# Second product of the first MoE with w_out as the stationary operand and 512 tokens moving

## The chip, the core and the metric

One NeuronCore of a Trainium2 chip runs the whole program in one launch. The metric is the device time of one execution in microseconds. Its engines run side by side, each in the order of its own list of instructions, and wait for one another by semaphores: TensorE (PE in the profile; PEld is its loading of stationary operands), VectorE (DVE), ScalarE (ACT), GpSimd (POOL) and SyncE (SP, which here only issues transfers). Matrix products are written to PSUM (eight banks of 512 float32 columns), everything else lives in SBUF or in device memory.

## The reference

Three stages follow each other. A linear attention with decay over 2 x 8 heads, 768 steps and head size 48 gives 1536 rows of 384 numbers. A dense layer then maps them through 2048 hidden values. Last comes a top-1 mixture of 8 experts.

```python
# stage 2: x is 1536 x 384
h = x @ w_in                                            # 384 x 2048
g = np.maximum(h, 0.0) + alpha * np.minimum(h, 0.0)
x = g @ w_out                                           # 2048 x 384
# stage 3: 8 experts, capacity 384 rows each
logits = x @ w_gate
expert_idx = np.argmax(logits, axis=1)
gate_w = softmax(logits)[row, expert_idx]
# rows go to their expert in order of the row number, up to the capacity
y = np.maximum(disp @ w1, 0.0) @ w2                     # 384 x 1024, 1024 x 384
out[i] = gate_w[i] * y[expert_idx[i], pos[i]]           # 0 for rows over the capacity
```

## The kernel before

The 1536 rows are treated as three blocks of four tiles of 128 rows. The attention turns each tile into x, transposed and split into a high and a low float32r part (`xT`), so that three products of parts stand for one float32 product (`PASS`: high x high, high x low, low x high).

The dense layer walks over 48 slices: for each of the three blocks, 16 slices of 128 hidden columns (`moe1_slice`, slice number g). In a slice TensorE makes the hidden values of 512 rows, nine matmuls with 512 moving columns (`moe1_first`, L599). ScalarE and VectorE apply the activation and split the result into `gh` and `gl` (128 hidden columns x 512 rows). Two slices later comes the second product (`moe1_second`, L584): for each of the four row tiles, a 128 x 128 piece of `gh` or `gl` is the stationary operand and a 128 x 384 piece of w_out moves; twelve matmuls a slice add into four PSUM banks `acc`, one for each row tile, with rows as partitions. TensorE's list is: hidden values of slice g, second product of slice g - 2, then whatever small work (attention of later tiles, routing of the block before) has been hung on the slice in the lists `work`.

When a block is done, its four banks are copied to `rows` by ScalarE (`evac`, L425). Routing then needs the logits. For each row tile TensorE transposes three pieces of `rows` (L431, the bank `px2`), a copy brings them to SBUF as `x2T` (L435), and six small matmuls against w_gate give 8 logits a row (L446, tile `pl`). For the first two blocks these steps are spread over the slices of the next block (`ROUTE_AT`). VectorE then picks the expert (`choose`, L454 to L466, one-hot `oh`), TensorE counts the rows of each expert before each row (`count`, L500, tile `pc`), VectorE works out the weight and the destination row (`weigh`, L475 to L488, and `place`, L506 to L515, destination `sl`), and GpSimd scatters each tile of 128 rows to the buffer `disp` in device memory by an indirect transfer (`scatter`, L522).

The last block has no later slices to hide in. Its routing is written out by hand after the loop (L1067 to L1117), in two halves of two row tiles, TA and TB, which share TensorE with `Early`: a product of expert 0 with 128 rows that are already there (tiles `eh_f`, `pht_f`, `ey_f`). After it come six matmuls whose result nobody reads (`keep_warm`, L756, tile `warm_e`). SP then loads the scattered rows of expert 0 (`load_rows`, L644), TensorE transposes them (`prep`, L658, tile `pd`), and the eight experts follow one after another (`expert`, L775 and L799), each while the weights of the next one are being split.

Of the kernel before, what the change touches and what calls it, by code (L numbers as in the profile page):

```python
# [18 lines left out]
P = 128  # L19
# [4 lines left out]
def kernel(  # L24
# [291 lines left out]
    ROUTE_AT = ((2, 4, 7, 10, 12, 13, 14),) * (NBLK - 2) + ((2, 3, 4, 5, 6, 7, 8),)  # L316
# [98 lines left out]
    def routing_steps(blk, R, s0, SUB, before=()):  # L415
# [7 lines left out]
        def evac(s):  # L423
            def f():
                nc.scalar.copy(R[:, s0 + s, 0:DM], accs[(blk, s0 + s)])  # L425
            return f

        def logit(s):
            pt = bank(f"px2_{nm}_{s}", "acc" if end else "att")
            for c in range(DC):  # L430
                nc.tensor.transpose(pt[:, c * P:(c + 1) * P], R[:, s0 + s, c * P:(c + 1) * P], ident)  # L431
            pool, tag = ((p1, "x2T"), (p2, "cv"), (p2, "cv"), (p1, "x2T"))[s0 + s if end else 0]
            T[s] = pool.tile([P, DC, P], F32, tag=tag, name=f"x2T{nm}_{s}")
            src = pt[:, 0:DM].rearrange("p (c t) -> p c t", c=DC)
            return lambda: (nc.vector.tensor_copy if end and s0 + s < 2 else nc.scalar.copy)(T[s], src)  # L435

        def logit_mm(s):
            if s == 0 and end:
                T["pl"] = bank(f"pl{nm}")
                T["lg"] = T["pl"][:, 0:SUB * E].rearrange("p (s e) -> p s e", s=SUB)  # L440
            elif s == 0:
                T["lg"] = p2.tile([P, SUB, E], F32, tag="lg", name=f"lg{nm}")
            pl = T["pl"][:, s * E:(s + 1) * E] if end else bank(f"pl{nm}_{s}")[:, 0:E]
            for c in range(DC):
                for x in range(2):
                    nc.tensor.matmul(pl[64 * x:64 * x + 64], T[s][:, c, 64 * x:64 * x + 64], wg[:, c, :],  # L446
                                     start=(c == 0), stop=(c == DC - 1), skip_group_check=True)
            return (lambda: None) if end else lambda: nc.vector.tensor_copy(T["lg"][:, s, :], pl)
# [116 lines left out]
        T["logit"], T["logit_mm"] = logit, logit_mm  # L565
        ev = [evac(s) for s in range(SUB)]
        T.update(choose=choose, weigh=weigh, count=count, place=place, scatter=scatter, total=total)
        steps = [pair(s) for s in range(SUB + 1)] + [lambda: weave(choose()), settle]
# [4 lines left out]
    gs = {}  # L573

    def moe1_second(fts, subs=None):
        blk = fts[0] // NFT
        for s in range(SIZES[blk]) if subs is None else subs:
            for g in fts:
                ft = g % NFT
                wout = moe1_w(ft // 2)[1]  # L580
                if ft == 0:
                    accs[(blk, s)] = ps_acc.tile([P, DM], F32, tag="acc", name=f"acc{blk}_{s}")
                for n, (a, b) in enumerate(PASS):
                    nc.tensor.matmul(accs[(blk, s)], gs[g][a][:, s * P:(s + 1) * P], wout[b][:, ft % 2, :],  # L584
                                     start=(ft == 0 and n == 0), stop=(ft == NFT - 1 and n == 2))
# [17 lines left out]
    def moe1_slice(g, work):  # L603
# [22 lines left out]
        if 2 <= g < NBLK * NFT - 1:  # L626
            moe1_second([g - 2])
# [18 lines left out]

    def claim(e):

        dT[e] = [p2.tile([P, DC, STRIDE], F32R, tag=("xh", "xl")[x], name=f"d{x}_{e}") for x in range(2)]
# [102 lines left out]
    def keep_warm(name, where, n, a, b):  # L752

        pt = bank(name, where)
        for _ in range(n):
            nc.tensor.matmul(pt[:, 0:b.free_size()], a, b, start=True, stop=True)  # L756
# [98 lines left out]
    with tc.manual_schedule():  # L855
# [190 lines left out]
        for blk in range(NBLK - 1):  # L1046
            def evac(blk=blk):
                ev, rt, _ = routing_steps(blk, rows_of(blk), 0, SIZES[blk])
# [20 lines left out]
        evA, rtA, TA = routing_steps(NBLK - 1, R, 0, 2)  # L1069
        evB, rtB, TB = routing_steps(NBLK - 1, R, 2, 2, before=(TA,))  # L1070
        L = [lambda T=T, s=s: T["logit"](s)() for T in (TA, TB) for s in range(2)]
        M = [lambda T=T, s=s: T["logit_mm"](s)() for T in (TA, TB) for s in range(2)]
        ev = evA + evB
        moe1_second([g - 2])
        moe1_second([g - 1], range(n - 1))
        for s in range(n - 1):
            moe1_second([g], [s])
            ev[s]()
        L[0]()
        moe1_second([g - 1], [n - 1])  # L1080
        L[1]()
        moe1_second([g], [n - 1])
        ev[3]()
        M[0]()
        L[2]()
        M[1]()
        L[3]()
        M[2]()
        early.hidden(0, 0, 1)
        weave(TA["choose"]())  # L1090
        TA["count"]()
        M[3]()
        early.hidden(0, 1, 9)
        weave(TA["weigh"](), TA["place"]())
        TA["scatter"]()
        weave(TB["choose"]())
# [9 lines left out]
        TB["total"]()  # L1106
# [7 lines left out]
        keep_warm("warm_e", "h", 6, early.d[0][:, 0, :], exp_w(0, 0)[0][:, 0, :])  # L1114
# [42 lines left out]
```

## Time and profile before

| | |
|---|---|
| median of three runs | 466.42 us (465.99 to 467.51) |
| profiled execution, its own time | 466.23 us |
| its span on the core | 464.5 us |
| mean granted TensorE clock | 0.989 of full |
| TensorE busy | 437.4 us (94% of the span) |
| VectorE, ScalarE, GpSimd busy | 271.0, 208.2, 157.7 us |

The span runs from the first to the last instruction of the program; the time of an execution is 1.7 us more. A row of the timeline gives the start in us from the start of the span, how long the row lasts, the engine, the source line, the operation, the tile written and the tiles read (stationary and moving operands are both named after the arrow), the shapes, and how many equal instructions stand in the row; in brackets is the idle time of the engine before it and what ended that. Matmuls overlap in the pipeline, so the pace of matmuls is read from start to start of rows, not from durations.

### The profile page before, as it was taken

To read this page: it belongs to the slowest core of one execution; us is meant where nothing else is said; L and a number is where in the kernel's file an instruction comes from. 1 tells how busy PE (TensorE), PEld (TensorE's weight loads), DVE (VectorE), ACT (ScalarE), POOL (GpSimd) and SP (SyncE) were. 2 spreads that over 40 slices of the span, in tenths; PEclk is the share of its full clock that TensorE was granted. 3 is DMA by queue.
4 is the path that set the end of the run, shared out by engine and by line. 5 is a ranking of instruction groups with operands and counts; after the bars stand their busy time and mean duration, and the time that the engine had idled before them with its cause. 6 is when DMAs were issued, how large, how long until landed. Compare 5 with 4: busy or idle time off the path is not lost. (4 is left out here: it accounts for less than half of the span.)

```text
span 464.5 us, 7861 instructions
## 1 busy us (share of the span) xinstructions
PE 437.4 (94%) x3039; PEld 385.1 (83%) x3039; DVE 271.0 (58%) x470; ACT 208.2 (45%) x344; POOL 157.7 (34%) x138
## 2 busy tenths in 40 slices
PE   7977799699899999999999999999999999999995
PEld 6766699588788988989988888987988889898884
DVE  6998998999753444445333665354463535452651
ACT  1236634354344333323244444336473646553761
POOL 6855457464440231100300030033343515241660
PEclk9999979989999999999999999999999999999999
DMA  6999950649610207101700020018956556580200
GB/s 129 229 281 250 318 157 4 183 158 361 172 30 15 52 2 233 57 0 43 299 1 1 0 87 0 1 56 290 382 178 239 188 169 212 172 271 35 72 10 25
DMA packets 70605, 62.28 MB, mean 134 GB/s; under 512 B 41935, under 2 KB 58239, under 8 KB 70561
## 3 DMA queue, kind: packets, MB, share of 16 engines
q1 hardware_dynamic: 68832, 57.29, 41.1%
q0 software_dynamic: 1728, 4.40, 2.5%
q8 instruction: 28, 0.46, 0.4%
q14 instruction: 17, 0.13, 0.1%
HBM read 49.99 MB, written 12.62 MB: 135 GB/s over the span
## 5 line engine op out<-in xcount | busy, mean ns | idle before, releaser
L584 PE MATMUL acc<-wm,gh 128*128 128x384 f32 x384 | 102.0, 347 | 0.5 <-POOL wm L368 0.5
L599 PE MATMUL h<-xh,wm 128*128 128x512 f32 (+1 forms) x294 | 86.2, 402 | 4.4 <-DVE gl L622 4.4
L618 DVE SCALAR_TENSOR_TENSOR h<-ng,sign,h 128x512 f32<-128x512 f32 x48 | 36.1, 752 | 68.2 <-ACT ng L615 68.2
L584 PEld LDWEIGHTS acc<-wm,gh 128*128 128x128 f32 x384 | 69.9, 191 | 4.7 <-POOL wm L368 0.8
L775 PE MATMUL eh<-we,d 128*128 128x512 f32 x252 | 65.1, 403 | 4.5 <-PEq L847 3.2
L584 PE MATMUL acc<-wm,gl 128*128 128x384 f32 x192 | 65.4, 341 | 0.0
L599 PEld LDWEIGHTS h<-xh,wm 128*128 128x128 f32 x294 | 52.6, 190 | 14.2 <-issue 2.8
L615 ACT ACTIVATE ng<-h,slope 128x512 f32<-128x512 f32 x48 | 33.1, 689 | 60.1 <-PE h L599 60.0
L775 PEld LDWEIGHTS eh<-we,d 128*128 128x128 f32 x252 | 45.7, 188 | 15.5 <-issue 4.4
L619 ACT CAST gh<-h 128x512 fp32r<-128x512 f32 x48 | 28.1, 586 | 60.8 <-DVE h L618 60.8
L674 ACT CAST we<-re 128x768 fp32r<-128x768 f32 x64 | 50.6, 839 | 9.6 <-DMA re<-in_moe_w_dram 6.8
L677 POOL TENSOR_TENSOR we<-re,we 128x768 fp32r<-128x768 f32 x21 | 40.6, 1932 | 38.5 <-ACT we L674 32.2
L790 DVE TENSOR_TENSOR hl<-pht,hh 128x512 fp32r<-128x512 f32 x28 | 19.4, 692 | 51.6 <-ACT hh L789 49.8
L368 POOL TENSOR_TENSOR wm<-rm,wm 128x768 fp32r<-128x768 f32 x16 | 32.2, 2013 | 47.4 <-ACT wm L367 43.6
L799 PE MATMUL ey<-we,hh 128*128 128x384 f32 x224 | 48.1, 346 | 0.0
L677 DVE TENSOR_TENSOR we<-re,we 128x768 fp32r<-128x768 f32 x43 | 40.3, 965 | 11.9 <-ACT we L674 8.9
L522 POOL DMA_INDIRECT disp<-rows,sl x12 | 12.6, 1051 | 99.9 <-DVE run L543 64.4
L599 PE MATMUL h<-xl,wm 128*128 128x512 f32 (+1 forms) x147 | 42.1, 395 | 0.1
L622 DVE TENSOR_TENSOR gl<-h,gh 128x512 fp32r<-128x512 f32 x48 | 33.0, 687 | 15.6 <-ACT gh L619 15.6
L799 PEld LDWEIGHTS ey<-we,hh 128*128 128x128 f32 x224 | 37.8, 189 | 0.3 <-ACT hh L789 0.3
L584 PEld LDWEIGHTS acc<-wm,gl 128*128 128x128 f32 x192 | 36.6, 191 | 0.0
L599 PEld LDWEIGHTS h<-xl,wm 128*128 128x128 f32 x147 | 27.7, 191 | 7.0 <-DVE xl L270 0.3
(181 smaller groups left out, 618.8 us busy)
## 6 DMA issues: line engine op xcount, KB each, us to landing
re<-in_moe_w_dram SPq DMA_DIRECT2D x32, 768.0 KB, 7.2
rm<-in_moe_w_in_dram SPq DMA_DIRECT2D x8, 768.0 KB, 8.1
rm<-in_moe_w_out_dram SPq DMA_DIRECT2D x8, 768.0 KB, 7.5
disp<-rowss SPq DMA_DIRECT2D x1, 4825.0 KB, 16.0
drow<-disp SPq DMA_DIRECT2D x7, 579.0 KB, 3.9
out_dram<-rowss SPq DMA_DIRECT2D x1, 2304.0 KB, 22.4
kn<-in_k_dram SPq DMA_DIRECT2D x10, 192.0 KB, 4.6
rn<-in_r_dram SPq DMA_DIRECT2D x10, 192.0 KB, 4.8
```

The source lines that it names most:

```text
L368: eng.tensor_tensor(lo, low.bitcast(F32), hi.bitcast(F32), ALU.subtract)
L584: nc.tensor.matmul(accs[(blk, s)], gs[g][a][:, s * P:(s + 1) * P], wout[b][:, ft % 2, :], start=(ft == 0 and n == 0), stop=(ft == NFT - 1 ...
L599: nc.tensor.matmul(phs[g][:, cols[0]:cols[1]], win[a][:, c, o:o + P], xs[b][:, c, cols[0]:cols[1]], start=(n == 0), stop=(n == 3 * DC - 1))
L615: nc.scalar.activation(ng, ph, AF.Relu, scale=slope[:, ft:ft + 1])
L618: nc.vector.scalar_tensor_tensor(ph, ng, sign[:, ft:ft + 1], ph, op0=ALU.mult, op1=ALU.add)
L619: nc.scalar.copy(gh, ph)
L622: nc.vector.tensor_tensor(gl, ph, gh.bitcast(F32), ALU.subtract)
L674: nc.scalar.copy(t[:, sl], src[:, sl])
L677: le.tensor_tensor(t[:, sl2], src[:, sl], t[:, sl].bitcast(F32), ALU.subtract)
L775: nc.tensor.matmul(ph[q], d[x][:, c, :], ww[y][:, c, :], start=(n == 0), stop=(n == 3 * DC - 1))
L790: nc.vector.tensor_tensor(hl, pt, hh.bitcast(F32), ALU.subtract)
L799: nc.tensor.matmul(py, hT[q][x][:, c * P:(c + 1) * P], ww[y][:, c, :], start=(q == 0 and not low and c == 0 and y == 0), stop=(q == 1 and ...
```

## The change

The second product now holds a 128 x 128 piece of w_out and moves 512 rows of `gh` or `gl`: nine matmuls a slice into three PSUM banks, one for each 128 of the 384 output columns, with output columns as partitions. The result is thus already transposed: ScalarE copies the three banks to a tile `x2T` (one for each block), the logits are made from it directly, and the rows that are scattered come from transposing it back (`turn_back`, tile `pR`, three transposes and one copy for each row tile, as many as before in the other direction). For the last block the two halves TA and TB become one group of four row tiles; the three banks are copied by ScalarE, VectorE and, in two halves of 256 columns, ScalarE. The six `keep_warm` matmuls of 512 columns become eighteen of 256, 224, 192, 160, 128 and 64 columns, three of each. `x2T` of the first block takes a buffer of the weight pool, that of the second and third a buffer of `xh`; expert 0 claims its own `xh` and `xl` buffers after the last block instead of 16 slices earlier.

```diff
-    ROUTE_AT = ((2, 4, 7, 10, 12, 13, 14),) * (NBLK - 2) + ((2, 3, 4, 5, 6, 7, 8),)
+    ROUTE_AT = ((2, 4, 7, 10, 13, 14),) * (NBLK - 2) + ((2, 3, 4, 5, 7, 8),)
...
-        def evac(s):
-            def f():
-                nc.scalar.copy(R[:, s0 + s, 0:DM], accs[(blk, s0 + s)])
-            return f
-
-        def logit(s):
-            pt = bank(f"px2_{nm}_{s}", "acc" if end else "att")
+        X2 = x2T[blk]
+
+        def evac(c):
+            nc.scalar.copy(X2[:, c], accs[(blk, c)])
+
+        def turn_back(s):
+            pt = bank(f"pR{nm}_{s}", "acc" if end else "att")
             for c in range(DC):
-                nc.tensor.transpose(pt[:, c * P:(c + 1) * P], R[:, s0 + s, c * P:(c + 1) * P], ident)
-            pool, tag = ((p1, "x2T"), (p2, "cv"), (p2, "cv"), (p1, "x2T"))[s0 + s if end else 0]
-            T[s] = pool.tile([P, DC, P], F32, tag=tag, name=f"x2T{nm}_{s}")
-            src = pt[:, 0:DM].rearrange("p (c t) -> p c t", c=DC)
-            return lambda: (nc.vector.tensor_copy if end and s0 + s < 2 else nc.scalar.copy)(T[s], src)
+                nc.tensor.transpose(pt[:, c * P:(c + 1) * P], X2[:, c, (s0 + s) * P:(s0 + s + 1) * P], ident)
+            return lambda: nc.scalar.copy(R[:, s0 + s, 0:DM], pt[:, 0:DM])
...
-                    nc.tensor.matmul(pl[64 * x:64 * x + 64], T[s][:, c, 64 * x:64 * x + 64], wg[:, c, :],
+                    o = (s0 + s) * P + 64 * x
+                    nc.tensor.matmul(pl[64 * x:64 * x + 64], X2[:, c, o:o + 64], wg[:, c, :],
...
-                then = []
-                if s > 0:
-                    then.append(logit_mm(s - 1))
-                if s < SUB:
-                    then.append(logit(s))
+                then = [logit_mm(s), turn_back(s)]
...
-                    nc.tensor.matmul(accs[(blk, s)], gs[g][a][:, s * P:(s + 1) * P], wout[b][:, ft % 2, :],
-                                     start=(ft == 0 and n == 0), stop=(ft == NFT - 1 and n == 2))
+                nc.tensor.matmul(accs[(blk, c)], wout[b][:, ft % 2, c * P:(c + 1) * P], gs[g][a],
+                                 start=(ft == 0 and n == 0), stop=(ft == NFT - 1 and n == 2))
...
+        half = n * P // 2
+        moe1_second(g - 2)
+        moe1_second(g - 1)
+        moe1_second(g, [0])
+        evac(nc.scalar.copy, 0)
+        moe1_second(g, [1])
+        evac(nc.vector.tensor_copy, 1)
+        moe1_second(g, [2])
+        evac(nc.scalar.copy, 2, 0, half)
+        evac(nc.scalar.copy, 2, half)
+        early.hidden(0, 0, 2)
+        for s in range(2):
+            T["logit_mm"](s)
+        early.hidden(0, 2, 3)
+        for s in range(2, n):
+            T["logit_mm"](s)
+        weave(T["choose"]())
+        back = [T["turn_back"](s) for s in range(2)]
+        early.hidden(0, 3, 6)
+        T["count"]()
+        for f in back:
+            f()
+        back = [T["turn_back"](s) for s in range(2, n)]
+        for f in back:
+            f()
+        early.hidden(0, 6, 9)
+        weave(T["weigh"](), T["place"]())
+        T["scatter"]()
         early.relu(0)
-        TB["count"]()
         early.hidden(1, 0, 5)
-        weave(TB["weigh"](), TB["place"]())
-        TB["scatter"]()
...
-        keep_warm("warm_e", "h", 6, early.d[0][:, 0, :], exp_w(0, 0)[0][:, 0, :])
+        keep_warm("warm_e", "h", 3, early.d[0][:, 0, :], exp_w(0, 0)[0][:, 0, :], (256, 224, 192, 160, 128, 64))
+        claim_rows(0)
```

TensorE's list after the last second product begins as follows before (acc is the second product, px a transposed row tile, pl the logits, eh_f the early product, pc the counts):

```order
L584 MATMUL acc_3_2392<-wm_1164,gh_15_2900 128x384 x2
L584 MATMUL acc_3_2392<-wm_1164,gl_15_2901 128x384
L446 MATMUL pl_0_2959<-wg,x2T_0_0_2944 64x8 x6
L431 MATMUL px_2_2_0_2966<-ident,rows_2906 128x128 x3
L446 MATMUL pl_0_2959<-wg,x2T_0_1_2953 64x8 x6
L431 MATMUL px_2_2_1_2978<-ident,rows_2906 128x128 x3
L446 MATMUL pl_2_2984<-wg,x2T_2_0_2970 64x8 x6
L722 MATMUL eh_f_2991<-we_0_2313,drow_f 128x512
L500 LDWEIGHTS upper_b
L500 MATMUL pc_0_3005<-oh_0_3002,upper_b 128x8
```

The same place of TensorE's list in the changed kernel (pR is a row tile turned back):

```order
L579 MATMUL acc_2_2284<-gh_15_2752,wm_1136 128x512 x2
L579 MATMUL acc_2_2284<-gl_15_2753,wm_1136 128x512
L721 MATMUL eh_f_2790<-we_0_2215,drow_f 128x512 x2
L444 MATMUL pl_0_2793<-wg,x2T_2254 64x8 x12
L721 MATMUL eh_f_2790<-we_0_2215,drow_f 128x512
L444 MATMUL pl_0_2793<-wg,x2T_2254 64x8 x12
L431 MATMUL pR_0_0_2833<-ident,x2T_2254 128x128 x3
L431 MATMUL pR_0_1_2837<-ident,x2T_2254 128x128 x3
L721 MATMUL eh_f_2790<-we_0_2215,drow_f 128x512 x3
L498 LDWEIGHTS upper_b
L498 MATMUL pc_0_2844<-oh_0_2830,upper_b 128x8
```

Before, the logits of two row tiles stand ahead of the choice that leads to the first counts; now those of all four do, and the rows come from the transposes behind them.

VectorE's list of the choice and the placing of TA before, from the logits to the operations that the first scatter waits for:

```order
L454 TENSOR_REDUCE mx_0_2993<-pl_0_2959 128x2
L458 SCALAR_TENSOR_TENSOR eq_0_2995<-pl_0_2959,mx_0_2993,rev 128x8 x2
L461 TENSOR_REDUCE mi_0_2998<-eq_0_2995 128x2
L463 TENSOR_TENSOR ex_0_3000<-pl_0_2959,mx_0_2993 128x16
L466 TENSOR_TENSOR oh_0_3002<-eq_0_2995,mi_0_2998 128x16
L475 TENSOR_SCALAR slot_0_3025<-mi_0_2998 128x2
L477 TENSOR_SCALAR mi_0_2998<-mi_0_2998 128x2
L506 TENSOR_TENSOR pe_0_3028<-pc_0_3005,oh_0_3002 128x16
```

The same place of VectorE's list in the changed kernel:

```order
L452 TENSOR_REDUCE mx_0_2819<-pl_0_2793 128x4
L456 SCALAR_TENSOR_TENSOR eq_0_2821<-pl_0_2793,mx_0_2819,rev 128x8 x4
L459 TENSOR_REDUCE mi_0_2826<-eq_0_2821 128x4
L461 TENSOR_TENSOR ex_0_2828<-pl_0_2793,mx_0_2819 128x32
L464 TENSOR_TENSOR oh_0_2830<-eq_0_2821,mi_0_2826 128x32
L473 TENSOR_SCALAR slot_0_2874<-mi_0_2826 128x4
L475 TENSOR_SCALAR mi_0_2826<-mi_0_2826 128x4
L504 TENSOR_TENSOR pe_0_2877<-pc_0_2844,oh_0_2830 128x32
```

The operations are the same, on four row tiles at once, with two more comparisons; a second run of them for TB no longer follows.

GpSimd's scatters of the last block, before:

```order
L522 DMA disp<-rows_1471,sl_0_2211 3200x386 x4
L522 DMA disp<-rows_2358,sl_0_2662 3200x386 x4
L522 DMA disp<-rows_2906,sl_0_3039 3200x386 x2
L522 DMA disp<-rows_2906,sl_2_3092 3200x386 x2
L684 DMA out_dram<-y_f,drow_f 1536x384
```

And in the changed kernel:

```order
L520 DMA disp<-rows_1423,sl_0_2121 3200x386 x4
L520 DMA disp<-rows_2255,sl_0_2535 3200x386 x4
L520 DMA disp<-rows_2758,sl_0_2888 3200x386 x4
L683 DMA out_dram<-y_f,drow_f 1536x384
```

The first two rows are those of the first two blocks; the last block's two pairs, each with its own destinations, have become one row of four with common destinations.

## Rows read from the trace of the kernel before

**Rows 1.** The page: busy time of TensorE, and its granted clock by slices.
```profile
PE 437.4 (94%) x3039; PEld 385.1 (83%) x3039; DVE 271.0 (58%) x470; ACT 208.2 (45%) x344; POOL 157.7 (34%) x138
...
PEclk9999979989999999999999999999999999999999
```

**Rows 2.** Timeline of TensorE, two slices: start us, us, engine, line, operation, tiles.
```profile
287.78 0.86 PE L599 MATMUL h<-xh,wm 128*128 128x512 f32 x3
...
289.88 0.51 PE L584 MATMUL acc<-wm,gh 128*128 128x384 f32 x2
...
291.97 0.87 PE L599 MATMUL h<-xh,wm 128*128 128x512 f32 x3
...
294.06 0.52 PE L584 MATMUL acc<-wm,gh 128*128 128x384 f32 x2
...
296.19 0.52 PE L584 MATMUL acc<-wm,gh 128*128 128x384 f32 x2
```

**Rows 3.** Timeline of TensorE, a routing step between two slices.
```profile
241.23 0.34 PE L584 MATMUL acc<-wm,gl 128*128 128x384 f32 x1
241.50 0.52 PE L446 MATMUL pl<-wg,x2T 128*64 128x8 f32 x12
241.95 0.55 PE L431 MATMUL px<-ident,rows 128*128 128x128 f32 x3
242.25 0.94 PE L599 MATMUL h<-xh,wm 128*128 128x512 f32 x3
```

**Rows 4.** Timeline of TensorE, from the last second product to expert 0.
```profile
300.90 0.33 PE L584 MATMUL acc<-wm,gl 128*128 128x384 f32 x1
...
302.08 0.52 PE L446 MATMUL pl<-wg,x2T 128*64 128x8 f32 x12
...
303.81 0.18 PE L500 MATMUL pc<-oh,upper_b 128*128 128x8 bf16 x1
...
303.92 0.17 PE L500 MATMUL pc<-run,ones_b 128*128 128x8 bf16 x1
...
314.14 1.56 PE L756 MATMUL warm_e<-we,drow_f 128*128 128x512 f32 x6
316.02 1.04 PE L658 MATMUL pd<-ident,drow 128*128 128x128 f32 x6 [0.32 <-DMA drow<-disp]
317.13 1.21 PE L775 MATMUL eh<-we,d 128*128 128x512 f32 x4
```

**Rows 5.** Timeline of GpSimd, the four scatters of the last block.
```profile
306.05 0.98 POOL L522 DMA_INDIRECT disp<-rows,sl  x1 [32.72 <-DVE ex L463]
307.33 0.99 POOL L522 DMA_INDIRECT disp<-rows,sl  x1 [0.30 <-DVE rows L482]
...
309.97 0.97 POOL L522 DMA_INDIRECT disp<-rows,sl  x1 [0.30 <-DVE counts L535]
```

**Rows 6.** Timeline of SP: loads of the rows of experts 0 and 1.
```profile
313.52 1.76 SPq L644 DMA_DIRECT2D drow<-disp  x4
```

**Rows 7.** Timeline of ScalarE: the last bank copied out.
```profile
301.26 0.48 ACT L425 COPY rows<-acc 128x384 f32<-128x384 f32 x1 [1.22 <-PE acc L584]
```

**Rows 8.** Timeline of VectorE, choice and placing of TA.
```profile
302.65 0.17 DVE L454 TENSOR_REDUCE mx<-pl 128x2 f32<-128x16 f32 x1 [1.35 <-PE pl L446]
302.86 0.36 DVE L458 SCALAR_TENSOR_TENSOR eq<-pl,mx,rev 128x8 f32<-128x8 f32 x2
...
303.46 0.17 DVE L466 TENSOR_TENSOR oh<-eq,mi 128x16 bf16<-128x16 f32 x1
...
304.13 0.17 DVE L506 TENSOR_TENSOR pe<-pc,oh 128x16 f32<-128x16 f32 x1 [0.21 <-PE pc L500]
...
305.13 0.16 DVE L488 RECIPROCAL rows<-sm 128x2 f32<-128x2 f32 x1
```

**Rows 9.** Stretches: busy us of each engine, then granted clock, DMA share, GB/s.
```profile
54.60:58.00 3.40, 1.74 (x12) 1.26 (x10) 3.40 (x6) 3.08 (x5) 1.63 (x1) 0.99 1.17 192
58.00:61.40 3.40, 3.40 (x51) 3.14 (x51) 3.37 (x4) 0.99 (x2) 3.40 (x3) 0.50 0.99 359
```

More of the change, by code (lines that the diff above doesn't have):

```diff
@@ L563, in pair @@
             return f
-        T["logit"], T["logit_mm"] = logit, logit_mm
-        ev = [evac(s) for s in range(SUB)]
+        T["turn_back"], T["logit_mm"] = turn_back, logit_mm
+        ev = [lambda c=c: evac(c) for c in range(DC)]
         T.update(choose=choose, weigh=weigh, count=count, place=place, scatter=scatter, total=total)
-        steps = [pair(s) for s in range(SUB + 1)] + [lambda: weave(choose()), settle]
+        steps = [pair(s) for s in range(SUB)] + [lambda: weave(choose()), settle]
         return ev, steps, T
@@ L573, with moe1_second @@
     gs = {}
[L575 to L583, printed above, removed]
-                    nc.tensor.matmul(accs[(blk, s)], gs[g][a][:, s * P:(s + 1) * P], wout[b][:, ft % 2, :],
-                                     start=(ft == 0 and n == 0), stop=(ft == NFT - 1 and n == 2))
+    x2T = {}
+    def moe1_second(g, cs=range(DC)):
+        blk, ft = g // NFT, g % NFT
+        wout = moe1_w(ft // 2)[1]
+        for c in cs:
+            if ft == 0:
+                accs[(blk, c)] = bank(f"acc{blk}_{c}", "acc")
+            for n, (a, b) in enumerate(PASS):
+                nc.tensor.matmul(accs[(blk, c)], wout[b][:, ft % 2, c * P:(c + 1) * P], gs[g][a],
+                                 start=(ft == 0 and n == 0), stop=(ft == NFT - 1 and n == 2))
     phs = {}
@@ L645, in load_rows, with claim_rows @@
         dsp[e] = t
+    def claim_rows(e):
+        dT[e] = [p2.tile([P, DC, STRIDE], F32R, tag=("xh", "xl")[x], name=f"d{x}_{e}") for x in range(2)]
     def claim(e):
-        dT[e] = [p2.tile([P, DC, STRIDE], F32R, tag=("xh", "xl")[x], name=f"d{x}_{e}") for x in range(2)]
+        if e > 0:
+            claim_rows(e)
         for q in range(NPIECE):
@@ L750, in out, with keep_warm @@
                                          stop=(q == 1 and low and c == HF // P - 1))
-    def keep_warm(name, where, n, a, b):
+    def keep_warm(name, where, n, a, b, widths=()):
         pt = bank(name, where)
-        for _ in range(n):
-            nc.tensor.matmul(pt[:, 0:b.free_size()], a, b, start=True, stop=True)
+        for w in widths or (b.free_size(),):
+            for _ in range(n):
+                nc.tensor.matmul(pt[:, 0:w], a, b[:, 0:w], start=True, stop=True)
     def expert_block(e, b, beside):
@@ L1068, with evac @@
         R = rows_of(NBLK - 1)
[L1069 to L1096, printed above, removed]
+        x2T[NBLK - 1] = x2T[NBLK - 2]
+        T = routing_steps(NBLK - 1, R, 0, n)[2]
+        def evac(eng, c, t0=0, t1=n * P):
+            eng(x2T[NBLK - 1][:, c, t0:t1], accs[(NBLK - 1, c)][:, t0:t1])
+        half = n * P // 2
+        moe1_second(g - 2)
+        moe1_second(g - 1)
[24 more added lines that the diff above has]
+        T["scatter"]()
         early.relu(0)
-        TB["count"]()
         early.hidden(1, 0, 5)
-        weave(TB["weigh"](), TB["place"]())
-        TB["scatter"]()
         early.turn(0)
@@ L1105 @@
         early.relu(1)
-        TB["total"]()
+        T["total"]()
         early.out(0, False, range(3))
```

6 lines of the change are left out of this document (5 added, 1 removed).

## The prediction

> **What bounds the kernel now.** I read the page first: TensorE is busy 94% of the span, and its granted clock is full in all but two of the 40 slices, both in the first quarter [rows 1]. So in the dense layer a change is worth what it takes from TensorE's own list, and elsewhere what it takes from the wait that ends last. The next view is TensorE's timeline. In two neighbouring slices the nine hidden matmuls of 512 columns take 2.10 and 2.09 us (287.78 to 289.88, 291.97 to 294.06), the twelve of the second product 2.09 and 2.13 (289.88 to 291.97, 294.06 to 296.19), with no idle time between [rows 2]. Third, the same view at the seam between the dense layer and expert 0: there TensorE does wait, 0.32 us for the rows of expert 0, and what stands ahead of that wait is six matmuls that nobody needs [rows 4]. So the seam is set by the rows. Their way back: SP issues the loads at 313.52, 2.50 before the first transpose at 316.02 [rows 4, 6]; it had to wait for the four scatters, which start at 306.05, 307.33, ... 309.97, one 1.28 after the other [rows 5]; the first of these waits for VectorE's choice and placing, from the logits at 302.65 to the weight at 305.13 [rows 8]. TensorE's last second product before that starts at 300.90 [rows 4].
>
> **The change part by part.** *The second product itself.* Nine matmuls of 512 columns are 4608 columns, twelve of 384 are 4608 as well. If columns set the pace, nothing is gained. The rows say so: mean 2.095 us for the nine, 2.11 for the twelve [rows 2]. The 0.015 between them is as large as the rounding; over 48 slices it would be 0.7 us at most, but in the first block TensorE also waits for others. I take -0.2. From both sides: the twelve alternate between 2.09 and 2.13 with the half of the w_out tile that moves, and what the new moving tile does to this no row shows. If all slices went at 2.09 it would be -1.0, all at 2.13 +1.0.
>
> The Trainium skill (TensorE: Matmul & The Clock Gate, Back-to-back issue gap) gives each matmul a fixed 2.5 ns beside its columns. As an estimate from that page, three matmuls fewer in 48 slices would be worth 0.36 us instead of my 0.2. The rows allow both.
>
> *Routing of the first two blocks.* Transposes (12 a block) and logit matmuls (24 a block) stay as many, in four places of a block instead of five. Entering such a place costs about 0.09: from the last product to the first logit matmul it is 0.27 (241.23 to 241.50) where a 384-column matmul takes 0.18 [rows 2, 3]. The way out costs about as much, but part comes back, since the transposes that stood alone now follow logits. I take -0.05 a block, -0.1 in all; bounds 0 and -0.4. Eight copies of 384 columns a block become three of 512 and four of 384 on ScalarE, which is busy 45% of the span [rows 1] and waited for by nobody there; that work is hidden.
>
> *The seam, step by step,* on the clock of the profile before. The last 36 products start at 294.06 [rows 2]; now they are 27 of 0.233, so TensorE is past them at 300.36. Two early matmuls (0.47) and the change of kind (0.09) bring it to 300.92. Four groups of logits at 0.45 (241.50 to 241.95 [rows 3]) and one early matmul between (0.23 and twice 0.09) bring it to 303.13. Does the copy of the third bank keep up? Its last matmul starts at 300.13 and lasts 0.39 (three in a row last 0.86 [rows 2]); a copy follows the end of a product by 0.03 (300.90 and 0.33, then 301.26 [rows 4, 7]), so it starts at 300.55. For 256 columns no row exists; 384 take 0.48 [rows 7], so at most 0.48 and in proportion 0.32; with 0.40 the first half is there at 300.95 and is wanted at 301.22 (eight of the first twelve matmuls later). The second is there by 301.5, wanted at 302.2. Covered, with 0.2 to spare.
>
> The choice before starts 0.11 after the logits' pace would let the next work start (302.08 and 0.45, then 302.65 [rows 4, 8]); so now at 303.24, 0.59 later than before, because it waits for four row tiles instead of two. It has two more comparisons, 0.18 each (two take 0.36 [rows 8]): +0.36. The one-hot starts 0.81 after the choice (302.65 to 303.46), now 303.24 + 0.81 + 0.36 = 304.41. Counts start 0.35 behind it (303.81), at 304.76; TensorE is there at 304.47, after two row tiles turned back and three early matmuls, so it waits and adds nothing. There are 14 counts instead of 5; five take 0.11 from first to last start (303.81 to 303.92 [rows 4]), so nine more are +0.25. From the first placing operation to the first scatter it is 1.92 (304.13 [rows 8] to 306.05 [rows 5]). Sum for the first scatter: 0.59 + 0.36 + 0.25 = +1.20, at 307.25.
>
> The rows themselves must be there too: four copies by ScalarE, the first behind the exponentials at about 304.7, then one each 0.53: the last at 306.9, still before the first scatter. Covered; without this cover each copy would be 0.5 late, but only for the scatter that needs it. Four scatters at 1.28 take 3.84 from first to last, where before it was 3.92. So the fourth starts at 311.09, +1.12. From there to the first transpose it was 6.05 (309.97 to 316.02), and the same transfers follow: 317.14.
>
> What falls away, the second choice and placing for TB, had been hidden: before, the fourth scatter came 2.64 after the second, hardly more than twice the 1.28 of GpSimd's own pace [rows 5]. The gain of the change, no copy between transposes and logits, is spent on waiting for four tiles. TensorE's own list cannot end later: 18 `keep_warm` matmuls have the 3072 columns of the six before; if each took the 0.1 of a transposed piece (241.95 to 242.25 for three [rows 3]) they would last 0.4 longer, and TensorE would be ready at about 316.1 instead of 315.7. It waits about 1.1 to 1.4 instead of 0.32.
>
> Nothing behind the seam is changed but buffers; all of it starts from these rows, so it shifts whole. Sum: -0.2 - 0.1 + 1.1 = +0.8 us. On the profiled execution (466.23, of which the span is 464.5) that is 467.0; on the median of the runs, 0.19 above it, 467.2. Forecast 467.1. The seam's own bounds: at best the rows come as early as TensorE is ready, which is -0.3 to 0; at worst the covers named above fail by 0.5, +1.6.
>
> **The rivals.** *The longer wait at the seam lowers the clock* (slower). After a wait of 1.66 us before 57.06, in a stretch in which TensorE was busy 1.74 of 3.40 us, the granted clock is 0.50, 1.2 GHz, for the next 3.4 us [rows 9]. The new wait of up to 1.4, six transposes, and 0.4 in which expert 0's first product waits for its operand (316.02 to 317.13 [rows 4]) look like that stretch. It would come from a wait about as long as that one on. Price: 3.4 us at half speed, where TensorE is the bound, lose 1.7: 468.8. The page bounds it: its two low slices of 11.6 us read 0.8 and 0.7, so a dip loses 1.2 to 3.5 [rows 1], 468.3 to 470.6. Against it: the matmuls that stand ahead keep TensorE busy to the last.
>
> The Trainium skill (TensorE: Matmul & The Clock Gate, PE-mode transpose) says that transposes do not count as busy for this clock. By that rule the six transposes lengthen the quiet stretch and the drop is likelier; no run here shows it.
>
> *The rows are not late.* If the chain is shorter than my sum, the seam is set by TensorE's list, and only the small gains stand: 466.42 - 0.3 - 0.2 = 465.9. For it: TensorE has less to wait for between logits. Against: each step of the sum has its row.
>
> *The moving tile sets the pace of the product.* All slices at 2.13: 467.1 + 1.2 = 468.3; all at 2.09: 467.1 - 0.8 = 466.3, and together with rows that are not late 465.1.
>
> *Fewer matmuls are worth more than the rows show,* the plain reading of the change: 3 of 12 dropped at an unchanged cost each would be 0.5 us a slice, 442. Against it: nine of 512 take as long as twelve of 384 [rows 2]. I give it 2%, mostly for a part of it.
>
> **How the numbers follow.** What a measurement of this kernel can tell from no change is about 0.3%, 1.4 us: faster is below 465.0, slower above 467.8. Forecast 0.58 (its own range 466.3 to 467.9, a tenth of it above 467.8); clock 0.15; rows not late 0.13; pace slow 0.07, fast 0.05; fewer matmuls 0.02. Faster: 0.02, half of the fast pace, and a part for what I do not see, together 0.11. Slower: 0.15 + 0.06 + 0.06 = 0.27. Within: 0.62. The range reaches from the rows in time with part of the fast pace, 465.3, to the clock's case, 468.8.
>
> **What would show it.** Nine second-product matmuls in 2.08 to 2.12 us a slice; logits of the last block done near 303; the first scatter about 1.2 later after the start of the last second products than before (there 11.99), and four at 1.28; the wait for `drow` ahead of the transposes above 1 us; the granted clock full behind it. Wrong would be a scatter that starts no later, a pace of the nine outside 2.05 to 2.15, or a time of the experts, from their first transpose on, that differs by more than 0.5 us.

## The result, and the profile after

The changed kernel takes 470.64 us (median of 7 runs, 468.33 to 471.15); before took 466.71 in the same group (7 runs, 465.99 to 468.17). The ratio of the mean times is 1.0069, with a 95% interval of 1.0045 to 1.0092. Two later groups of the same two kernels gave 1.0052 and 1.0046 (experiments 5 and 12), so this is the largest of three. The forecast was 467.1 with a range from 465.3 to 468.8, with 0.27 for slower. The profiled execution took 470.71 us with a span of 468.8, 4.3 longer than the span before.

First the page of the changed kernel: busy time of the engines, and the granted clock in 40 slices.

```profile
PE 437.3 (93%) x2907; PEld 364.7 (78%) x2907; DVE 269.8 (58%) x453; ACT 207.8 (44%) x342; POOL 157.0 (33%) x138
...
PEclk9999999999999999999999999997999999999999
```

TensorE is as busy as before with 132 fewer matmuls [rows 1]. A slice with a 7 stands where there was none, at 316 to 328 us; the low slices before were early, at 58 to 70 and 93 to 105. The timeline of TensorE, from one of the last slices to expert 0, shows where that is.

```profile
289.96 0.63 PE L579 MATMUL acc<-gh,wm 128*128 128x512 f32 x2
...
292.06 0.86 PE L594 MATMUL h<-xh,wm 128*128 128x512 f32 x3
...
294.16 0.63 PE L579 MATMUL acc<-gh,wm 128*128 128x512 f32 x2
...
300.46 0.63 PE L721 MATMUL eh_f<-we,drow_f 128*128 128x512 f32 x2
301.02 0.87 PE L444 MATMUL pl<-wg,x2T 128*64 128x8 f32 x24
...
303.06 0.88 PE L431 MATMUL pR<-ident,x2T 128*128 128x128 f32 x6
...
304.53 0.17 PE L498 MATMUL pc<-oh,upper_b 128*128 128x8 bf16 x1
...
313.64 2.11 PE L756 MATMUL warm_e<-we,drow_f 128*128 128x256 f32 x18
317.80 1.89 PE L657 MATMUL pd<-ident,drow 128*128 128x128 f32 x6 [2.04 <-DMA drow<-disp]
319.33 5.62 PE L775 MATMUL eh<-we,d 128*128 128x512 f32 x14
324.79 0.60 PE L784 MATMUL pht<-ident,hs 128*128 128x128 f32 x4
```

Nine second products take 2.10 a slice (289.96 to 292.06), and the logits are done at 303.06: both as forecast. The last line but two answers to the 0.32 of [rows 4]: TensorE waits 2.04 us for the rows. Behind it the matmuls are slow; 14 first products of expert 0 take 5.46 from first start to the transposes (319.33 to 324.79). The stretches around it (columns: us, busy time of each engine, granted clock, share and rate of the transfers):

```profile
313.70:317.10 3.40, 2.05 (x19) 1.94 (x17) 0.62 (x1) 0.00 (x0) 0.97 (x1) 1.00 0.25 61
317.20:320.60 3.40, 2.73 (x9) 2.13 (x10) 0.93 (x2) 1.36 (x3) 0.00 (x0) 0.50 0.96 315
320.60:324.00 3.40, 3.40 (x9) 2.63 (x9) 2.01 (x3) 1.44 (x3) 0.00 (x0) 0.50 0.98 335
324.00:327.40 3.40, 3.40 (x22) 2.96 (x22) 0.69 (x1) 2.50 (x5) 1.83 (x1) 1.00 1.05 393
```

The granted clock is 0.50, that is 1.2 GHz, for 6.8 us behind the wait. The first, third and fourth scatter on GpSimd, and SP's loads of the rows:

```profile
307.04 0.97 POOL L520 DMA_INDIRECT disp<-rows,sl  x1 [33.61 <-ACT rows L432]
...
309.59 0.97 POOL L520 DMA_INDIRECT disp<-rows,sl  x1 [0.30 <-DVE counts L533]
310.87 0.97 POOL L520 DMA_INDIRECT disp<-rows,sl  x1 [0.31 <-issue]
```

```profile
315.31 1.80 SPq L639 DMA_DIRECT2D drow<-disp  x4
```

The fourth scatter starts 0.90 later than before (309.97, [rows 5]), SP's load 1.79 later (313.52, [rows 6]). So the 4.3 us of the span are: start of the last products +0.10; fourth scatter against that start +0.80; from the scatter to the first transpose 6.93 instead of 6.05, +0.88; from that transpose to the first product of expert 0 1.53 instead of 1.11, +0.42; its first 14 products +2.08. Of these, 1.78 are rows that come later and 2.5 are the clock. From the end of the 14 products to the end of the span it is 144.0 in both.

What holds the load 0.88 longer behind the scatter? SP's load waits for the whole scatter: it starts 0.86 behind the end of the scatter's last packet, and in 11 of the 14 profiles of this document 0.81 to 0.86 behind it. The next rows are transfers that begin in two short stretches of the changed kernel: 312.3 to 312.7, and 313.7 to 315.0 (packets, size, rate; then each queue with its share of the 16 engines' time).

```profile
q0 software_dynamic: 34, 0.09, 63.1%
q8 instruction: 1, 0.02, 22.4%
...
DMA packets 4, 0.00 MB, mean 4 GB/s; under 512 B 2, under 2 KB 3, under 8 KB 4
q0 software_dynamic: 4, 0.00, 2.7%
```

Amid the packets of the fourth scatter (q0) one packet of 16 KB of the queue "instruction" begins, at 312.50, and takes 1.44 us. All but four of the scatter's packets end by 312.94; these four begin when the large packet ends, at 313.94, and end by 314.45, as packets do that stand behind it on one DMA engine. In all five profiles with one group of four, `keep_warm` and no added small matmuls (this one and experiments 1, 2, 5 and 12) the scatter's last packet ends 0.51 behind the end of the large one, which takes 0.94 to 1.44. Such a packet comes 28 times in the kernel before, 27 times in the changed one, which has fewer matmuls: we take it to be TensorE's code, and the experiments that only add matmuls do move it. Before the change it came at 310.92, 0.95 behind the fourth scatter's start; now 1.63 behind it.

### The profile page after: what moved, and what is told of

Same layout as the page of the kernel before. It is cut to its first block, busy times and chain, and to the rows that moved or that the text cites. A ratio compares the mean times of both kernels' runs of the same rounds, so it can differ in the third digit from the quotient of the medians.

```text
span 468.8 us, 7577 instructions
## 1 busy us (share of the span) xinstructions
PE 437.3 (93%) x2907; PEld 364.7 (78%) x2907; DVE 269.8 (58%) x453; ACT 207.8 (44%) x342; POOL 157.0 (33%) x138
## 5 line engine op out<-in xcount | busy, mean ns | idle before, releaser
L579 PE MATMUL acc<-gh,wm 128*128 128x512 f32 x288 | 92.6, 402 | 0.4 <-POOL wm L368 0.4
L775 PE MATMUL eh<-we,d 128*128 128x512 f32 x252 | 67.3, 413 | 4.3 <-PEq L847 3.2
L579 PEld LDWEIGHTS acc<-gh,wm 128*128 128x128 f32 x288 | 52.8, 188 | 14.1 <-POOL wm L368 1.1
L775 PEld LDWEIGHTS eh<-we,d 128*128 128x128 f32 x252 | 47.4, 195 | 15.5 <-issue 4.3
L579 PE MATMUL acc<-gl,wm 128*128 128x512 f32 x144 | 57.0, 396 | 0.0
L579 PEld LDWEIGHTS acc<-gl,wm 128*128 128x128 f32 x144 | 27.0, 188 | 6.3
```

Source lines behind the costliest of these rows:

```text
L579: nc.tensor.matmul(accs[(blk, c)], wout[b][:, ft % 2, c * P:(c + 1) * P], gs[g][a], start=(ft == 0 and n == 0), stop=(ft == NFT - 1 and n ...
L775: nc.tensor.matmul(ph[q], d[x][:, c, :], ww[y][:, c, :], start=(n == 0), stop=(n == 3 * DC - 1))
```

## The experiments

Theory: late rows make a wait, and the wait lets the clock fall. Rivals: the fall comes from the narrow `keep_warm` matmuls; the new product itself costs time; later, that the late landing has a cause of its own. Each kernel was timed beside the one before; ratios are of mean times, to that one. What is read from each profile, in rows like those above, stands together in a table below.

**1. The wait filled.**

```diff
         keep_warm("warm_e", "h", 3, ..., (256, 224, 192, 160, 128, 64))
+        keep_warm("warm_m", "h", 8, early.d[0][:, 0, :], exp_w(0, 0)[0][:, 0, :])
```

> The changed kernel with eight more matmuls of 512 columns (about 1.87 us, result read by nobody) behind the eighteen of keep_warm, so that TensorE works through most of the 2.04 us in which it waited for drow. Theory (the idle wait lets the clock fall): the idle time before pd is about 0.2 us, pd starts where it did (the rows set it, about 317.8), the granted clock stays full behind it, the 14 first products of expert 0 take about 3.4 us instead of 5.46, and the time is about 468.1, 2.5 less than the changed kernel. Rival A (the fall comes from elsewhere, such as the transposes or the narrow matmuls themselves): the clock falls all the same, about 470.6. Rival B (the new matmuls delay the transposes): pd later than 318.0 and no gain.

467.44 us, ratio 1.0027 (1.0017 to 1.0037), and no fall:

```profile
315.91 2.11 PE L756 MATMUL warm_m<-we,drow_f 128*128 128x512 f32 x8
317.99 0.55 PE L657 MATMUL pd<-ident,drow 128*128 128x128 f32 x3
318.78 0.55 PE L657 MATMUL pd<-ident,drow 128*128 128x128 f32 x3 [0.24 <-DMA drow<-disp]
319.11 3.55 PE L775 MATMUL eh<-we,d 128*128 128x512 f32 x14
322.49 0.60 PE L784 MATMUL pht<-ident,hs 128*128 128x128 f32 x4
```

The 14 products take 3.38 again, though the transposes start as late as in the changed kernel. The theory holds, with a time 0.7 below its 468.1; what remains (1.2 us over before) goes with the late rows.

**2. The wide `keep_warm` in the changed kernel** (six of 512 columns again, and nothing else).

```diff
-        keep_warm("warm_e", "h", 3, ..., (256, 224, 192, 160, 128, 64))
+        keep_warm("warm_e", "h", 6, early.d[0][:, 0, :], exp_w(0, 0)[0][:, 0, :])
```

> The changed kernel with the former keep_warm: six matmuls of 512 columns instead of eighteen narrow ones of the same 3072 columns. Theory (the wait for late rows lets the clock fall): the wait before pd stays at 1.9 to 2.4 us, the clock falls as before, the time is 470 to 471. Rival (the narrow matmuls let the clock fall, the wait does not): clock full at the seam, about 468.1.

468.89 us, ratio 1.0048 (1.003 to 1.0066). In its profile (468.44 us) the wait is the longer one, and the clock stays:

```profile
314.22 1.56 PE L756 MATMUL warm_e<-we,drow_f 128*128 128x512 f32 x6
318.08 1.09 PE L657 MATMUL pd<-ident,drow 128*128 128x128 f32 x6 [2.30 <-DMA drow<-disp]
319.20 3.54 PE L775 MATMUL eh<-we,d 128*128 128x512 f32 x14
```

Neither expectation fits: the wait came, the fall did not, and the time lies between. So a wait of this length doesn't always lower the clock. The six runs spread from 466.94 to 469.62; whether the clock fell in the slower ones no profile shows.

**3. The kernel before without its `keep_warm`.**

```diff
-        keep_warm("warm_e", "h", 6, early.d[0][:, 0, :], exp_w(0, 0)[0][:, 0, :])
```

> The kernel before without its six keep_warm matmuls (1.56 us of TensorE whose result nobody reads); rows and all else as before. Theory (an idle wait of about 1.9 us ahead of the transposes is enough for the clock to fall): idle before pd 1.9 instead of 0.32, pd where it was (316.0), clock at half behind it, time about 469.2, 2.5 more than before. Rival (the fall needs something of the changed kernel, its layout or its later rows): no fall, 466.7.

467.11 us, ratio 1.0011 (0.9998 to 1.0024): no difference that can be told. The wait was 1.79, the clock full. The theory's number missed here too.

**4. The changed product, the last block in two halves.** Choice, counts and scatters of the first two row tiles run as soon as their logits are there; `keep_warm` is wide.

```diff
-        T = routing_steps(NBLK - 1, R, 0, n)[2]
+        TA = routing_steps(NBLK - 1, R, 0, 2)[2]
+        TB = routing_steps(NBLK - 1, R, 2, 2, before=(TA,))[2]
...
+            TA["logit_mm"](s)
+        weave(TA["choose"]())
+        early.hidden(0, 2, 3)
+        for s in range(2):
+            TB["logit_mm"](s)
+        TA["count"]()
...
+        weave(TA["weigh"](), TA["place"]())
+        TA["scatter"]()
```

> The changed product (w_out held, 512 tokens moving) with the last block's routing again in two halves: choice, counts and scatters of the first two row tiles as soon as their logits are there, and the former six wide keep_warm matmuls. Theory (the group of four makes the rows late, that makes the wait, and the wait lowers the clock): first scatter at 305.4 to 306.0 instead of 307.04, fourth near 309.3, wait before pd at most 0.4, clock full, time 466.0 to 466.7. Rival (the new product's layout itself costs time, or the wait comes from the transfer and not from the scatters' start): 468 or more.

464.95 us (5 runs, 464.79 to 465.38), ratio 0.9967 (0.9954 to 0.998): faster than both other kernels, and below the 466.0 to 466.7 that were expected. The product's layout is not the loss. The scatters and SP's loads:

```profile
304.13 0.98 POOL L520 DMA_INDIRECT disp<-rows,sl  x1 [31.88 <-DVE ex L461]
```

```profile
310.90 3.53 SPq L639 DMA_DIRECT2D drow<-disp  x4
```

The first scatter starts 11.13 behind the last 27 products' start (293.00), earlier even than before (11.99). Yet the transposes start only 22.02 behind it: here the 16 KB packet falls among SP's loads (at 311.92), and their issue takes 3.53 instead of 1.76.

**5. The changed kernel again.** 

> The changed kernel once more, beside the other kernels of this group. Theory (narrow keep_warm together with the wait lets the clock fall in most executions): most runs at 469.8 to 471.2 with the fall, a minority at 468.3 to 468.9 without, median about 470; where the profile shows the fall, expert 0's 14 first products take 5.4 us, else 3.4. Rival (the changed kernel is slow by something that the other variants also have): median 468 to 469, as with wide keep_warm matmuls.

468.47 us (467.44 to 470.39), ratio 1.0052 (1.0034 to 1.0071), as with wide `keep_warm`: the rival's number, not the theory's 470. Its profile, the fastest of these runs, shows a wait of 1.42 and no fall.

**6. Narrow `keep_warm` in the kernel before** (the line of experiment 2 the other way round).

> The kernel before with the changed kernel's eighteen narrow keep_warm matmuls instead of six of 512 columns; rows as early as before, so next to no idle wait ahead of the transposes (pd about 0.25 later, since the eighteen last 2.1 us instead of 1.6). Theory A (the clock falls only where narrow matmuls and the wait for late rows come together): clock full, 466.3 to 466.8. Theory B (narrow matmuls are enough): the clock falls behind them in most runs, 468.5 to 469.0.

466.03 us, ratio 0.9997 (0.9985 to 1.001), clock full. Theory A holds: the narrow matmuls by themselves cost nothing.

**7. Wide `keep_warm`, and the code packet moved** by twelve small matmuls in `total`.

```diff
                                                op0=ALU.min, op1=ALU.subtract)
+                for _ in range(12):
+                    nc.tensor.matmul(pt[:, 64:64 + E], ones_b, run, start=True, stop=True)
                 return
```

> The changed kernel with the former six wide keep_warm matmuls and, about 4 us ahead of them, twelve more matmuls of 8 columns (0.3 us, result read by nobody), which move TensorE's 16 KB loads of code some 2 us earlier against the rest. Theory (the fourth scatter lands late because a 16 KB packet of code occupies one DMA engine at 312.5 to 312.9): the code packet comes near 311, SP's load of the rows follows the fourth scatter by 3.5 to 3.7 us as before the change, not by 4.1 to 4.4, the wait before pd is 0.3 to 0.7 shorter than with wide keep_warm alone (2.30), and the time 0.4 to 0.7 less. Rival (scatters that follow each other at 1.28 land later by themselves): still 4.1 or more, same time.

466.35 us, ratio 0.9999 (0.9988 to 1.001). The packet began 0.52 behind the fourth scatter's start, and the load followed the scatter by 3.26. That was more than expected, and two things were mixed, since the twelve waited 0.61 for VectorE:

```profile
310.20 0.44 PE L537 MATMUL ptot<-run,ones_b 128*128 128x8 bf16 x12 [0.61 <-DVE counts L534]
...
317.01 1.03 PE L659 MATMUL pd<-ident,drow 128*128 128x128 f32 x6 [0.26 <-DMA drow<-disp]
```

TensorE was busy later, and there was hardly a wait left. Experiment 9 takes the two apart.

**8. Two halves with the same twelve matmuls, and two wide `keep_warm` matmuls instead of six.** 

> The changed product with the last block's routing in two halves, the same twelve small matmuls, and two instead of six wide keep_warm matmuls. In the version without them the code packet came at 311.9, between SP's loads of the rows, SP's third load took 2.18 us, and the rows were there 7.0 us after the fourth scatter. Theory (the code packet delays the rows): packet near 310.3, rows there 5.3 to 6.0 us after the fourth scatter, TensorE's own list then ends about as early (13.9 us shorter wait not needed), pd 0.7 to 1.2 us earlier than without (22.0 us after the start of the last 27 products), time 464.0 to 464.5. Rival (the rows' way is not shortened): wait before pd of about 1 us instead of 0.42, same time, 464.8 to 465.3, or 467 if the clock falls.

(The words in brackets on a wait of 13.9 us are a slip and stand for nothing.) 465.13 us, ratio 0.9981 (0.9966 to 0.9995). The packet came at 309.55, SP's loads took 1.76, and the transposes started 21.24 behind the last products, 0.8 earlier than in experiment 4, without a wait. So the rows' way is shorter, as the theory has it, but the time is the rival's: it is no better than experiment 4's (0.9967).

**9. As 7, with the twelve matmuls where they wait for nothing.**

```diff
                 self.py = bank("ey_f", "acc")
+                for _ in range(12):
+                    nc.tensor.matmul(self.py[:, DM:DM + E], ones_b, run, start=True, stop=True)
```

> The changed kernel with six wide keep_warm matmuls and twelve matmuls of 8 columns (result read by nobody) ahead of the early second product, written so that they wait for nothing; they move TensorE's code packet ahead of the third scatter. The early work of TensorE ends at most 0.3 us later than with wide keep_warm alone, so a wait for the rows stays. Theory (the code packet makes the last scatter land late, and the wait then lets the clock fall in a part of the executions): SP's load 3.0 to 3.3 us after the fourth scatter instead of 4.12, wait before pd 0.8 to 1.4 instead of 2.30, time 1.0 to 2.5 less than with wide keep_warm alone, at 1.001 to 1.003 of before. Rival (the gain of the earlier shifted version came only from a busier TensorE): load still 3.8 to 4.4 behind the scatter, 1.005 of before.

466.24 us (465.88 to 467.01), ratio 1.0012 (1.0003 to 1.0021). The packet begins at 310.38, later than meant (the third scatter starts at 308.96) but ahead of the packets of the fourth scatter; the first rows below are the transfers that begin in 310.2 to 310.6. Below them, the fourth scatter, SP's load, and TensorE's wait.

```profile
q0 software_dynamic: 13, 0.04, 29.7%
q8 instruction: 1, 0.02, 24.1%
```

```profile
310.24 0.97 POOL L520 DMA_INDIRECT disp<-rows,sl  x1 [0.30 <-issue]
```

```profile
313.56 1.76 SPq L639 DMA_DIRECT2D drow<-disp  x4
```

```profile
315.94 1.02 PE L657 MATMUL pd<-ident,drow 128*128 128x128 f32 x6 [1.07 <-DMA drow<-disp]
317.06 3.54 PE L777 MATMUL eh<-we,d 128*128 128x512 f32 x14
```

The load follows the scatter by 3.32, as the theory has it (3.0 to 3.3), and a wait of 1.07 stays, with a full clock. By the two ratios, twelve matmuls more make the kernel of experiment 2 0.36% faster, 1.7 us. In the two profiles 0.95 of that is the earlier first transpose (22.41 for 23.36); that the rest are falls of the clock in other runs of experiment 2 is not shown.

**10. The changed kernel without `keep_warm`.** 

> The changed kernel without its keep_warm matmuls, so that TensorE is idle for 3.5 to 4.2 us ahead of pd. Theory (idle time ahead of the transposes is what lets the clock fall, with a chance that grows with its length): the clock is at half behind the wait in the profile and in nearly every execution, expert 0's 14 first products take 5.4 us or a large part of them does, 1.009 to 1.012 of before. Rival (the fall in the first profile of the changed kernel was a rare event, and the loss has another cause): clock full in the profile, no more than 1.006 of before.

468.61 us, ratio 1.006 (1.0042 to 1.0078). The clock fell in its profile, but for 3.4 us, and the ratio is below the theory's 1.009: here the packet came 3.17 behind the scatter, and the first rows landed early again (load 3.16 behind). TensorE waited twice, 2.75 and 1.17.

```profile
315.66 0.55 PE L657 MATMUL pd<-ident,drow 128*128 128x128 f32 x3 [2.75 <-DMA drow<-disp]
317.38 0.77 PE L657 MATMUL pd<-ident,drow 128*128 128x128 f32 x3 [1.17 <-DMA drow<-disp]
317.80 4.96 PE L775 MATMUL eh<-we,d 128*128 128x512 f32 x14
```

**11. Two halves, seven small matmuls in the place of experiment 9, two wide `keep_warm`.** 

> The changed product, the last block in two halves, two wide keep_warm matmuls, and seven matmuls of 8 columns that wait for nothing ahead of the early second product, to move the code packet between the last scatter's packets and SP's loads. Theory: packet at 2.0 to 2.4 us after the fourth scatter, SP's load at 2.9 to 3.1, its four issues in 1.8 us instead of 3.53, pd 20.6 to 20.9 us after the start of the last 27 second products (in two halves alone 22.0, before the change 21.95), time 0.995 to 0.997 of before. Rival (the rows' way has a length of its own): pd at 21.2 or later, 0.997 to 0.999.

464.18 us (463.74 to 465.8), ratio 0.9965 (0.9952 to 0.9978). The time is the theory's, the way there is not: in the profile, its slowest run, the packet came at 1.90 and not behind 2.0, the load followed by 4.21, and the transposes started at 21.69.

**12. The changed kernel a third time.** 

> The changed kernel a third time, for a third profile and for its spread beside the others of this group. Theory (scatters 0.8 later, a landing that varies with the code packet, and a fall of the clock in some executions): pd 22.9 to 23.7 us after the start of the last 27 second products; with the fall expert 0's first products take 5.4 us and the time is 469.5 to 471.5, without it 3.4 and 467.3 to 468.9; median 1.005 to 1.008 of before. Rival (a constant loss): all runs within 0.5 us of each other.

467.76 us (467.01 to 469.19), ratio 1.0046 (1.003 to 1.0061). The runs spread over 2.2 us, so the loss is not a constant one. A wait of 1.83, and again a fall, for 3.4 us:

```profile
314.60:318.00 3.40, 1.57 (x14) 1.24 (x13) 0.00 (x0) 0.11 (x1) 0.97 (x1) 1.00 0.60 179
318.10:321.40 3.30, 3.30 (x10) 2.48 (x9) 2.66 (x4) 2.21 (x4) 0.00 (x0) 0.50 0.96 311
```

All profiles together, in us. *Scatter*: start of the first one behind the start of the last second products. *Packet* and *load*: start of the 16 KB packet, and of SP's load, behind the start of the fourth scatter. *Wait*: TensorE's idle time ahead of the first transpose. *pd*: start of that transpose behind the start of the last second products.

| kernel | ratio | scatter | packet | load | wait | pd | clock at half |
|---|---|---|---|---|---|---|---|
| before | 1 | 11.99 | 0.95 | 3.55 | 0.32 | 21.95 | no |
| changed | 1.0069 | 12.88 | 1.63 | 4.44 | 2.04 | 23.63 | 6.8 us |
| 5, changed | 1.0052 | 12.88 | 1.50 | 3.81 | 1.42 | 23.02 | no |
| 12, changed | 1.0046 | 12.88 | 1.58 | 4.25 | 1.83 | 23.42 | 3.4 us |
| 1, wait filled | 1.0027 | 12.88 | 1.68 | 4.28 | 0 | 23.53 | no |
| 2, wide | 1.0048 | 12.88 | 1.45 | 4.12 | 2.30 | 23.36 | no |
| 7, wide, moved | 0.9999 | 12.88 | 0.52 | 3.26 | 0.26 | 22.37 | no |
| 9, wide, moved | 1.0012 | 12.88 | 0.14 | 3.32 | 1.07 | 22.41 | no |
| 10, no warm | 1.006 | 12.88 | 3.17 | 3.16 | 2.75, then 1.17 | 22.40 | 3.4 us |
| 3, before, no warm | 1.0011 | 11.99 | 1.36 | 4.13 | 1.79 | 22.49 | no |
| 6, before, narrow | 0.9997 | 11.99 | 1.12 | 3.92 | 0.18 | 22.37 | no |
| 4, two halves | 0.9967 | 11.14 | 3.95 | 2.92 | 0.42 | 22.02 | no |
| 8, halves, moved | 0.9981 | 11.14 | 1.90 | 3.00 | 0 | 21.24 | no |
| 11, halves, moved | 0.9965 | 11.14 | 1.90 | 4.21 | 1.18 | 21.69 | no |

## Why the prediction was wrong

**The product and the routing of the first blocks (-0.3) were worth nothing.** The pace was right: 2.10 a slice. From the hidden matmuls of the first block's last slice to the start of the last second products, TensorE's starts are 128.97 and 294.06 before, 129.10 and 294.16 now: 165.09 and 165.06. Over the 29 slices from the second block's first second product on, the three profiles with the old product take 148.25 and the eleven with the new one 148.21, so the gain there is 0.04; the 0.36 that the prediction worked out beside its own 0.2 is not borne out either. The start itself varies by more than 0.3 from profile to profile of the same code (292.67 to 294.72 over these kernels), so what the first block adds cannot be told. Nothing of the loss comes from here.

**The scatters (+1.12) were sized a little too high.** The fourth is 0.80 later against the start of the last products. The choice came when forecast (303.18 for 303.24), but the counts followed the one-hot by 0.24 instead of 0.35, and the one-hot the choice by 1.11 instead of 1.17; only from the first placing operation to the scatter it was longer, 1.98 for 1.92. The cover of the four row copies held barely: ScalarE's last ends at 306.31, VectorE's last operation at 306.28, and the scatter starts 0.76 behind the latter (before, 0.75). The mechanism stands: four row tiles must have their logits before any row has a place.

**"From there to the first transpose it was 6.05, and the same transfers follow" failed.** In three profiles of the changed kernel it was 6.93, 6.32 and 6.71. The transfers are the same, but not what they meet: with another number of matmuls on TensorE, and with scatters 0.9 later, the 16 KB packet fell among the packets of the fourth scatter. In all eight profiles in which it began 0.95 to 1.68 behind the scatter's start, the load came 3.55 to 4.44 behind it; in the four in which it began before 0.6 or after 3 us, 2.92 to 3.32. At 1.90 both were seen; in experiment 11 the load came 1.35 behind the scatter's last packet, and what held it is not shown. The kernel before had the same hit, only a lighter one. This step was worth 0.3 to 0.9 us, and experiment 9 shows that moving the packet gives all of it back: there it was 5.70. In experiment 5's profile, without a fall, the first transpose came 23.02 behind the last products, where the forecast has 23.08 (317.14 less 294.06). That is luck: the forecast has the fourth scatter 0.3 too late and the way from there 0.3 too short.

**The clock was a rival with 0.15, priced at 1.7 us; it is the largest part.** "The matmuls that stand ahead keep TensorE busy to the last" was the argument against it. They ended where forecast (315.76), but the rows came later than forecast (317.80 for 317.14), and the wait was 1.4 to 2.0 instead of 1.1 to 1.4. Where the clock fell for 6.8 us it cost 2.5 (0.42 ahead of the first product and 2.08 in the 14); the 3.4 us of experiment 12 cost 1.36 (first 14 products in 4.74, from 318.42 to 323.16, instead of 3.38). The forecast's price lay between these, but it came from half of the fall that it was read from. The stretch behind the last of [rows 9] was at half clock too, so that fall went on to 64.6:

```profile
61.40:64.80 3.40, 3.40 (x12) 3.40 (x12) 3.37 (x6) 2.08 (x5) 3.09 (x3) 0.50 0.76 155
```

Filling the wait (experiment 1) leaves the late rows and removes the fall; with the packet moved (experiments 7 and 9) the rows are early, the wait is short, and there is no fall either. One profile each would be thin, but the times agree: of the 22 runs of the changed kernel 13 took more than 468.5 us, of the 35 runs of experiments 1, 7 and 9 none. So the fall of the changed kernel needs the wait; that is shown. How often it comes is not: two of three profiles, and runs spread over 467.0 to 471.2. What decides at a given wait stays open: at this place waits of 1.83, 2.04 and 2.75 (with 1.17 more behind it) had a fall behind them, 1.79 and 2.30 had none, and no shorter one had.

The Trainium skill (TensorE: Matmul & The Clock Gate, HAM oscillation — how this bites in real kernels) describes a kernel whose clock drops again and again because its matmuls wait for a transfer. This case agrees as to kind: 2.04 us of waiting for `drow`, then 0.50 of the clock; experiment 2, with 2.30 and a full clock, shows that it need not happen. To the rule of the Trainium skill on transposes that the prediction named (TensorE: Matmul & The Clock Gate, PE-mode transpose), one thing can be added: where six of them followed TensorE's work with no wait ahead (experiments 1 and 8), the clock stayed full.

So the sum for the profiled execution is +0.1 (start), +0.8 (scatters), +0.9 (packet), +2.5 (clock). The forecast had -0.3, +1.1, 0 and 0. Its sign was right, and so was its mechanism for the scatters; it failed at two steps that it held to be unchanged (the landing) or unlikely (the clock), and the second of these is the larger part of the loss.

Why two halves are 0.3% faster than before is shown only in part. Their first scatter is 0.85 earlier than before, and in experiments 8 and 11 the transposes start 0.7 and 0.3 earlier; in the profile of experiment 4 they don't, and its 1 us lies in an early start of the dense layer's end (293.00), which varies by itself.

## What to carry to other kernels

A change that only saves instructions on a full engine can still move everything that hangs on their number: ask what else comes in step with the list, and where it will land. Where an engine already waits a little, a chain that feeds it should get its first part early; a group of four that is a little cheaper in all was worse here than two of two. And a wait on TensorE is not priced by its length alone: add what the clock may do behind it.

## What the runs showed of the hardware

- One 16 KB packet of the queue "instruction" took 0.9 to 1.6 us at this place. Packets of a scatter behind it started when it ended (313.94), and SP's load, which waits for the whole scatter, started 0.86 after the last of them: up to 1.5 us later than without it (load 4.44 against 2.92 behind the scatter, the changed kernel and experiment 4).
- Twelve matmuls of 8 columns, 0.30 us of TensorE, moved that packet from 1.45 to 0.14 behind the scatter (experiments 2 and 9).
- The clock fell for 3.4 or for 6.8 us, and a wait of 2.30 could pass without a fall where one of 1.83 did not.
- Matmuls of 64 to 256 columns with as many columns in all as six of 512 took 0.55 longer (2.11 and 1.56), and by themselves changed neither clock nor time.
